# Decode attention on one core: K transposed by VectorE in blocks of bf16 pairs instead of on TensorE

## The chip, the cores and the metric

The kernel runs on one core of a Trainium2 chip. The time is device microseconds of one execution on that core. The engines are named as in the profile: PE (TensorE matmul), PEld (TensorE weight load), DVE (VectorE), ACT (ScalarE), POOL (GpSimd), SP (SyncE).

## What is computed

Softmax attention of one query position over 65,536 keys, with 32 query heads sharing 8 key heads, four to each, and head size 128, in bf16:

```python
B, Hq, Hkv, Sq, Sk, D = 1, 32, 8, 1, 65536, 128
k = jnp.repeat(k, rep, axis=1)          # rep = 4
v = jnp.repeat(v, rep, axis=1)
scores = jnp.einsum("bhqd,bhkd->bhqk", q, k) * D ** -0.5
p = softmax(scores, axis=-1)
out = jnp.einsum("bhqk,bhkd->bhqd", p, v)
```

K and V are 134.2 MB each and are read once. Each key takes part in four dot products and four weighted sums, so there is little arithmetic for each byte.

## The kernel before

K and V are cut into chunks of 128 x 64 keys (2 MB). Chunk i belongs to key head h = i // 8; partition p of a chunk holds 64 keys in a row (16 KB), so a tile is the t-th key of each of the 128 partitions, 128 keys x 128 elements. There are N = 64 chunks of K and as many of V, C = 8 to a head.

SP issues all loads in one order, worked out ahead (`merged`): K chunks run C chunks ahead of V chunks, and at the end V falls further behind. K has four buffers (NK), V six (NV). A K load waits until the chunk four back has been transposed (`tr_s`, L163), a V load until the values of the chunk six back are done (`pv_s`, L167). The first K chunk and the last V chunk come in pieces (FIRST, LAST).

For the scores PE needs the head dimension on the partitions, while a tile arrives with the keys there. So for each group of 8 tiles PE makes eight transposes into a PSUM bank (`trb`, L211), DVE or ACT copies the bank to SBUF (`ktb`; DVE L283, ACT L332, shared out by `on_act`), and PE makes eight matmuls with the transposed tile as weights and the four query columns as moving operand (`qkb`, L224). PE's order is written out in `pe_ops`: scores trail the transposes by three groups, and eight value matmuls (`PV`) go between. ACT moves a chunk's 256 columns of scores from PSUM to `scs` (L340), DVE takes their maximum for each query head (L287). After a head's last chunk DVE combines the maxima (L294), POOL reduces over partitions (L182), ACT scales the result (L344) and makes four exponentials into `pts`, with their sums (L353), and POOL sums over partitions (L184).

The values of a head add up in PSUM over its chunks: for heads 0 to 6 the V tile is the weight and four columns of `pts` move (L252); for head 7 `pts` is the weight and the V tile's 128 columns move (L254). DVE divides by the sum (L306; the last head L317). Heads 0 to 6 are transposed once on PE (L259) and stored from ACT's queue; head 7 is stored from SP's.

Of the kernel before, what the change touches and what calls it, by code (L numbers as in the profile page):

```python
# [1 line left out]

# [6 lines left out]
DT = mybir.dt  # L9
# [5 lines left out]
T = 64  # L15
TB = 8
G = T // TB
NK, NV = 4, 6
NTR = 4
NKT = 8  # L20
LAG = 3
FIRST = (16, 16, 32)
LAST = (32, 16, 8, 8)


def bass_standalone__gqa_softmax__decode_kernel(nc, q, k, v, out):
    B, Hq, Sq, D = q.shape
    _, H, Sk, _ = k.shape
    assert B == 1 and Sq == 1 and D == P and Hq % H == 0
    R = Hq // H  # L30
    CK = P * T
    assert Sk % CK == 0 and R * T <= 512 and Hq <= P
    C = Sk // CK
    TPH = C * T
    N = H * C
    scale = float(D) ** -0.5
# [5 lines left out]
    def merged(ahead):  # L42

        items = [(float(j), 0, ("K", j)) for j in range(N)]
        for i in range(N):
            back = 0.5 * max(0, i - (N - 2 * C)) if i < N - C else 0.5 * C
            items.append((i + C - ahead + back, 1, ("V", i)))
        return [it for _, _, it in sorted(items)]

    dma_seq, pe_seq = merged(0), merged(-1)  # L50


    pe_ops = []
    j = 0
    pend = []

    def tr(kg):
        pe_ops.append(("TR", kg))
        pend.append(kg)
        if len(pend) > LAG:  # L60
            pe_ops.append(("QK", pend.pop(0)))

    while j < len(pe_seq):
        kind, i = pe_seq[j]
        both = kind == "K" and j + 1 < len(pe_seq) and pe_seq[j + 1][0] == "V"
        last_k = kind == "K" and i == N - 1
        if kind == "K":
            for g in range(G):
                tr(i * G + g)
                if both and not last_k:  # L70
                    pe_ops.append(("PV", pe_seq[j + 1][1], g))
            if last_k:
                while pend:
                    pe_ops.append(("QK", pend.pop(0)))
                both = False
        else:
            for g in range(G):
                pe_ops.append(("PV", i, g))
        j += 2 if both else 1


    def on_act(kg):
        kc, g = divmod(kg, G)
        if kc < C:
            return g in (1, 4, 6)
        return kc % C >= 2 and g in (1, 5)

    n_act = [0]
    for kg in range(N * G):
        n_act.append(n_act[-1] + on_act(kg))  # L90
# [9 lines left out]
    ktb = [sb(f"ktb{i}", [P, TB * P], DT.bfloat16) for i in range(NKT)]  # L100
    scs = [sb(f"scs{i}", [P, TPH * R], DT.float32) for i in range(2)]
    pts = [sb(f"pts{i}", [P, TPH * R], DT.bfloat16) for i in range(2)]
    qsb = sb("qsb", [Hq, D], DT.bfloat16)
    qT = sb("qT", [P, Hq], DT.bfloat16)
    ident = sb("ident", [P, P], DT.bfloat16)
    identf = sb("identf", [R, R], DT.float32)
    hpart = sb("hpart", [P, 2 * C * R], DT.float32)
# [9 lines left out]
    orows = sb("orows", [Hq - R, D], DT.bfloat16)  # L117
    olast = sb("olast", [R, D], DT.bfloat16)
    warm = sb("warm", [P, 2], DT.float32)

    trb = [S(nc.psum_tensor(f"trb{i}", [P, TB * P], DT.bfloat16)) for i in range(NTR)]
    qkb = [S(nc.psum_tensor(f"qkb{i}", [P, 512], DT.float32)) for i in range(2)]
    pvb = [S(nc.psum_tensor(f"pvb{i}", [P, 512], DT.float32)) for i in range(2)]

    def sem(name):
# [6 lines left out]
    q_in, id_in, o_out = sem("q_in"), sem("id_in"), sem("o_out")  # L132
    tr_s, cpd_s, cpa_s = sem("tr_s"), sem("cpd_s"), sem("cpa_s")
    qk_s, sc_s, mx_s, hm_s = sem("qk_s"), sem("sc_s"), sem("mx_s"), sem("hm_s")
    hma_s, nb_s, ex_s, ls_s = sem("hma_s"), sem("nb_s"), sem("ex_s"), sem("ls_s")
    pv_s, rc_s, fin_s = sem("pv_s"), sem("rc_s"), sem("fin_s")
    qt_s, qT_s, idf_s, ot_s, or_s, warm_s = (
        sem("qt_s"), sem("qT_s"), sem("idf_s"), sem("ot_s"), sem("or_s"), sem("warm_s"))
# [10 lines left out]

    eye = nc.inline_tensor(np.eye(P).astype(ml_dtypes.bfloat16), name="eye").ap()  # L150
# [4 lines left out]
    def _(sp):  # L155
# [19 lines left out]
        sp.wait_ge(o_out, 32)  # L175

    @block.gpsimd
    def _(g):
        for h in range(H):
            hs = slice(h * R, (h + 1) * R)  # L180
            g.wait_ge(hm_s, h + 1)
            g.partition_all_reduce(hmaxa[:, hs], hmax[:, hs], P, bass.bass_isa.ReduceOp.max).then_inc(hma_s, 1)  # L182
            g.wait_ge(ex_s, R * (h + 1))
            g.partition_all_reduce(lsum[:, hs], rsum[:, hs], P, bass.bass_isa.ReduceOp.add).then_inc(ls_s, 1)  # L184

    @block.tensor
    def _(pe):
        def copied(kg):
            if on_act(kg):
                pe.wait_ge(cpa_s, n_act[kg + 1])  # L190
            else:
                pe.wait_ge(cpd_s, kg + 1 - n_act[kg + 1])

        pe.wait_ge(id_in, 16)
        pe.wait_ge(q_in, 16)
        pe.transpose(qkb[1][:, 0:Hq // 2].bitcast(DT.bfloat16), qsb[:, :], ident[0:Hq, 0:Hq]).then_inc(qt_s, 1)  # L196
        for op in pe_ops:
            if op[0] == "TR":
                kg = op[1]
                kc, g = divmod(kg, G)  # L200
                if kc == 0:
                    for n, a, b in pieces(FIRST):
                        if a == g * TB:
                            pe.wait_ge(first_in[n], 16)
                elif g == 0:
                    pe.wait_ge(k_in[kc % NK], 16 * (kc // NK + (kc % NK > 0)))
                if kg >= NTR:
                    copied(kg - NTR)
                for t in range(TB):
                    at = (g * TB + t) * D  # L210
                    ins = pe.transpose(trb[kg % NTR][:, t * P:(t + 1) * P], kbuf[kc % NK][:, at:at + D], ident[:, :])  # L211
                ins.then_inc(tr_s, 1)
            elif op[0] == "QK":
                kg = op[1]
                kc, g = divmod(kg, G)
                h = kc // C
                copied(kg)
                if kg == 0:
                    pe.wait_ge(qT_s, 1)
                if g == 0 and kc >= 2:  # L220
                    pe.wait_ge(sc_s, kc - 1)
                for t in range(TB):
                    at = (g * TB + t) * R
                    ins = pe.matmul(  # L224
                        qkb[kc % 2][:, at:at + R],
                        lhsT=ktb[kg % NKT][:, t * P:(t + 1) * P],
                        rhs=qT[:, h * R:(h + 1) * R],
                        start=True, stop=True,
                    )
                if g == G - 1:  # L230
                    ins.then_inc(qk_s, 1)
            else:
                _, i, g = op
                h, c = divmod(i, C)
                if g == 0:
                    if c == 0:
                        pe.wait_ge(ex_s, R * (h + 1))
                        if h >= 2:
                            pe.wait_ge(fin_s, h - 1)
                    if i < N - 1:  # L240
                        pe.wait_ge(v_in[i % NV], 16 * (i // NV + 1))
                if i == N - 1:
                    for n, a, b in pieces(LAST):
                        if a == g * TB:
                            pe.wait_ge(last_in[n], 16)
# [14 lines left out]


    side = []
    for op in pe_ops:
        if op[0] == "TR":
            side.append(("CP", op[1]))
        elif op[0] == "QK" and op[1] % G == G - 1:
# [123 lines left out]
```

## Time and profile before

Three executions took 655.04, 657.07 (the median) and 657.52 us. The profiled one:

| | |
|---|---|
| its own time | 654.79 us |
| its span, first to last instruction | 653.0 us |
| mean granted clock of PE | 0.658 |
| busy: PE, PEld | 606.0 us (93%), 602.4 us (92%) |
| busy: DVE, ACT, POOL | 313.6 us (48%), 178.5 us (27%), 6.6 us (1%) |
| instructions | 25,665, of them 12,290 matmuls |
| moved by DMA | 270.12 MB, 414 GB/s over the span |
| 2 MB loads, issue to landing | K 27.4 us, V 32.1 us (median) |
| SP's K loads waiting for transposes (`tr_s`) | 515.3 us in 60 waits, the longest 12.4 us |

How to read it. A page divides the span into 40 slices of 16.3 us; a digit is the busy share of a slice in tenths, and PEclk is the clock that was granted to PE, in tenths of full speed. A row of a group gives line, engine, operation, output and inputs, shape and count; then busy time and mean nanoseconds of one; then the idle time before it and what ended most of it. Durations of neighbours can overlap, so the distance between the starts of two instructions is read from the timeline (start, length, engine, line, operation). SP's waits cost nothing as long as loads issued earlier are still moving.

### The profile page before, as it was taken

What the parts mean: (1) busy time and instruction counts of PE and PEld (TensorE: products, weight loads), DVE (VectorE), ACT (ScalarE), POOL (GpSimd) and SP (SyncE); (2) the same over time, 40 slices, a digit from 0 to 9 for tenths busy, and PEclk for the clock granted to TensorE, in tenths of its full rate; (3) what the DMA queues carried; (4) which work ended last, traced back from release to release, by engine and by line L of the source; (5) the groups of instructions that cost most, each with busy time, mean ns of one, the idle gap of its engine ahead of it and who ended that gap; (6) DMA issues with size and microseconds to landing.
All of it is one profiled execution on the core that took longest, in us unless ns stands there. A gap on an engine that the chain in (4) does not pass through costs nothing.

```text
span 653.0 us, 25665 instructions
## 1 busy us (share of the span) xinstructions
PE 606.0 (93%) x12290; PEld 602.4 (92%) x12290; DVE 313.6 (48%) x497; ACT 178.5 (27%) x246; POOL 6.6 (1%) x20
## 2 busy tenths in 40 slices
PE   5987898998798989999999999999999999998798
PEld 5987898998798989999999999999999999988697
DVE  3666544564444734446444464444644446455200
ACT  3555122232222322223122231222312223132400
POOL 0000000000000000000000000000000000000000
PEclk9999858776866755555555555555555555597799
DMA  8999999999999999999999999999999999899995
GB/s 359 429 424 425 426 423 425 427 428 422 427 428 423 423 426 427 426 424 428 424 424 425 425 426 425 425 426 424 429 423 426 428 391 387 360 426 428 386 425 206
DMA packets 19497, 270.12 MB, mean 414 GB/s; under 512 B 2370, under 2 KB 2370, under 8 KB 3010
## 3 DMA queue, kind: packets, MB, share of 16 engines
q1 hardware_dynamic: 19160, 268.45, 97.4%
q8 instruction: 96, 1.57, 1.0%
q10 hardware_dynamic: 234, 0.05, 0.0%
q14 instruction: 7, 0.06, 0.0%
HBM read 268.48 MB, written 0.01 MB: 411 GB/s over the span
## 4 chain that ended last, share of the span: by engine, by line
PE 75%; DMA 20%; issue 3%; ACT 1%; DVE 1%; SPq 0%; POOL 0%; DVEq 0%
PE trb L211 49%; DMA kbuf<-in_k_dram 17%; PE pvb L252 12%; PE qkb L224 12%; DMA vbuf<-in_v_dram 3%; PE pvb L254 2%; ACT pts L353 1%; DVE ktb L283 1%; SPq L160 0%; DVE hpart L287 0%; SPq L164 0%; POOL hmaxa L182 0%; DVE olast L317 0%; DVE hmax L294 0%; ACT negb L344 0%
## 5 line engine op out<-in xcount | busy, mean ns | idle before, releaser
L211 PE MATMUL trb<-ident,kbuf 128*128 128x128 bf16 x4096 | 451.9, 279 | 20.3 <-DMA kbuf<-in_k_dram 15.0
L283 DVE COPY ktb<-trb 128x1024 bf16<-128x1024 bf16 x404 | 277.2, 690 | 289.3 <-PE trb L211 286.4
L211 PEld LDWEIGHTS trb<-ident,kbuf 128*128 128x128 bf16 x4096 | 342.4, 125 | 23.0 <-DMA kbuf<-in_k_dram 15.7
L332 ACT ACTIVATE ktb<-trb 128x1024 bf16<-128x1024 bf16 x108 | 110.6, 1024 | 348.5 <-PE trb L211 348.5
L224 PE MATMUL qkb<-qT,ktb 128*128 128x4 bf16 x4096 | 195.6, 170 | 7.5 <-issue 7.3
L224 PEld LDWEIGHTS qkb<-qT,ktb 128*128 128x128 bf16 x4096 | 194.7, 109 | 6.5 <-issue 6.1
L252 PE MATMUL pvb<-pts,vbuf 128*128 128x4 bf16 x3584 | 153.2, 166 | 9.9 <-issue 7.2
L252 PEld LDWEIGHTS pvb<-pts,vbuf 128*128 128x128 bf16 x3584 | 126.4, 102 | 11.3 <-issue 8.4
L340 ACT ACTIVATE scs<-qkb 128x256 f32<-128x256 f32 x64 | 24.5, 383 | 73.9 <-PE qkb L224 73.9
L353 ACT ACTIVATE pts<-scs,negb 128x512 bf16<-128x512 f32 x32 | 41.1, 1435 | 0.3
L287 DVE TENSOR_REDUCE hpart<-scs 128x4 f32<-128x256 f32 x64 | 38.9, 608 | 0.9 <-ACT scs L340 0.9
L254 PE MATMUL pvb<-vbuf,pts 128*4 128x128 bf16 x512 | 30.3, 223 | 1.5 <-DMA vbuf<-in_v_dram 0.9
L254 PEld LDWEIGHTS pvb<-vbuf,pts 128*4 128x4 bf16 x512 | 29.8, 87 | 1.9 <-DMA vbuf<-in_v_dram 1.1
L317 DVE TENSOR_SCALAR olast<-pvb,rcol 4x128 bf16<-4x128 f32 x1 | 0.3, 338 | 25.7 <-PE pvb L254 25.7
L182 POOL PARTITION_ALL_REDUCE hmaxa<-hmax x8 | 3.0, 372 | 564.5 <-DVE hmax L294 564.5
L353 ACT ACTIVATION_READ_ACCUMULATOR pts<-scs,negb 128x1 f32 x32 | 8.2, 255 | 0.0
L306 DVE TENSOR_TENSOR oT<-pvb,recip 128x4 bf16<-128x4 f32 x7 | 1.1, 161 | 10.4 <-PE pvb L252 10.2
L196 PE MATMUL qkb<-ident,qsb 32*128 32x32 bf16 x1 | 0.2, 181 | 5.6 <-DMA qsb<-in_q_dram 5.6
L196 PEld LDWEIGHTS qkb<-ident,qsb 32*128 32x128 bf16 x1 | 0.1, 97 | 5.6 <-issue 5.6
L344 ACT ACTIVATE negb<-hmaxa 128x4 f32<-128x4 f32 x8 | 1.6, 205 | 11.0 <-POOL hmaxa L182 11.0
L184 POOL PARTITION_ALL_REDUCE lsum<-rsum x8 | 3.4, 431 | 44.0 <-ACT pts L353 44.0
L309 DVE COPY orows<-trb 28x128 bf16<-28x128 bf16 x1 | 0.2, 214 | 5.5 <-PE trb L259 5.5
(14 smaller groups left out, 5.7 us busy)
## 6 DMA issues: line engine op xcount, KB each, us to landing
kbuf<-in_k_dram SPq DMA_DIRECT2D x63, 2048.0 KB, 27.4
vbuf<-in_v_dram SPq DMA_DIRECT2D x63, 2048.0 KB, 32.1
kbuf<-in_k_dram SPq DMA_DIRECT2D x2, 512.0 KB, 4.5
kbuf<-in_k_dram SPq DMA_DIRECT2D x1, 1024.0 KB, 7.1
vbuf<-in_v_dram SPq DMA_DIRECT2D x1, 1024.0 KB, 17.6
vbuf<-in_v_dram SPq DMA_DIRECT2D x1, 512.0 KB, 18.5
vbuf<-in_v_dram SPq DMA_DIRECT2D x2, 256.0 KB, 18.7
ident<-eye ACTq DMA_DIRECT2D x1, 32.0 KB, 3.2
```

The lines of the kernel that those rows point to most:

```text
L182: g.partition_all_reduce(hmaxa[:, hs], hmax[:, hs], P, bass.bass_isa.ReduceOp.max).then_inc(hma_s, 1)
L184: g.partition_all_reduce(lsum[:, hs], rsum[:, hs], P, bass.bass_isa.ReduceOp.add).then_inc(ls_s, 1)
L211: ins = pe.transpose(trb[kg % NTR][:, t * P:(t + 1) * P], kbuf[kc % NK][:, at:at + D], ident[:, :])
L224: ins = pe.matmul(qkb[kc % 2][:, at:at + R], lhsT=ktb[kg % NKT][:, t * P:(t + 1) * P], rhs=qT[:, h * R:(h + 1) * R], start=True, stop=True,)
L252: ins = pe.matmul(pvb[h % 2][:, 0:R], lhsT=v_t, rhs=p_t, start=st, stop=sp_)
L254: ins = pe.matmul(pvb[h % 2][0:R, 0:D], lhsT=p_t, rhs=v_t, start=st, stop=sp_)
L283: dv.tensor_copy(ktb[n % NKT][:, :], trb[n % NTR][:, :]).then_inc(cpd_s, 1)
L287: dv.tensor_reduce(hp[:, h % 2, c, :], scs[h % 2][:, c * T * R:(c + 1) * T * R].rearrange("p (t g) -> p g t", g=R), AX.X, ALU.max,).then_i ...
L332: ac.activation(ktb[n % NKT][:, :], trb[n % NTR][:, :], AF.Copy).then_inc(cpa_s, 1)
L340: ac.activation(scs[s][:, c * T * R:(c + 1) * T * R], qkb[n % 2][:, 0:T * R], AF.Copy).then_inc(sc_s, 1)
L344: ac.activation(negb[:, hs], hmaxa[:, hs], AF.Copy, scale=-scale).then_inc(nb_s, 1)
L353: ac.activation(pv[:, g_, :], sv[:, g_, :], AF.Exp, bias=negb[:, col], scale=scale, accum_out=rsum[:, col],).then_inc(ex_s, 1)
```

## The change

Chunks become 128 x 128 keys (4 MB, 32 KB in each partition): T = 128, N = 32 chunks, C = 4 to a head. K has two buffers, V three, of twice the size.

A group is now 16 tiles. DVE reads the group as int32, that is as pairs of bf16, and transposes it in one instruction of 128 x 1024 int32, block by block of 32 x 32, from SBUF to SBUF (`ktb`, four buffers). Within a quarter of 32 partitions the pairs of the head dimension come to lie on the partitions; the four quarters hold four different sets of keys. So a tile of `ktb`'s columns, taken every second bf16 (e = 0 or 1) and for each half b of the pairs, has 32 pair indices of four key sets on its 128 partitions. The query is spread into `qblk`, block-diagonal: for each head, b and e, 16 columns, of which the four columns of set a are non-zero only on quarter a. Four matmuls (b, e) add up to 16 columns of scores for 128 column positions. ACT then sorts the scores back: for each half chunk (a unit of 4 groups) sixteen moves, each from one quarter of `qkb` to one quarter of `scs`. `qkb` has six banks.

PE has no transposes and `trb` is gone; ACT makes no copies of K. PE makes a group's scores, then the 16 values of the V chunk that lies beside (`beside`), in order; the last five V chunks (`rest`) follow after all K. DVE waits for a unit's moves and takes the maximum after the second group of the next unit, and at the end of a head at once. POOL clears `qblk`, `oT` and `identf` at the start and makes the identity; the identity's load is gone, and q is loaded four times from ACT's queue, once into each quarter. Heads 0 to 6 are transposed at the end by DVE (`oX`) and stored in four pieces from ACT's queue.

The load order is now K0 K1 K2 V0 K3 V1 K4 V2 and so on to V23, and then K26 K27 V24 K28 K29 V25 K30 V26 K31 V27 V28 V29 V30 V31. A K load waits for the transposes of the chunk two back, a V load for the values of the chunk three back. Maximum, exponentials, values and division have the form they had, with the same number of exponentials and maxima.

```diff
-T = 64
-TB = 8
-G = T // TB
-NK, NV = 4, 6
-NTR = 4
-NKT = 8
-LAG = 3
-FIRST = (16, 16, 32)
-LAST = (32, 16, 8, 8)
+S4 = 32
+T = 128
+TG = 16
+G = T // TG
+U = 2
+GU = G // U
+NK, NV = 2, 3
+NKT = 4
+NQ = 6
+FIRST = (16, 16, 32, 64)
+LAST = (64, 32, 16, 8, 8)
...
+    def behind(i):
+        late = i - (N - 2 * C)
+        return i + C - 2 if late < 0 else min(N - 1, i + C - 2 + (1, 2, 2, 3)[min(late, 3)])
+
+    dma_seq = []
+    for j in range(N):
+        dma_seq.append(("K", j))
+        dma_seq += [("V", i) for i in range(N) if behind(i) == j]
...
+    for i in range(N):
+        j = max(free, i + C, behind(i) + 1)
+        if j < N:
+            beside[j] = i
+            free = j + 1
         else:
+            rest.append(i)
...
+        def scores(kg):
...
+            kt = ktb[kg % NKT][:, :].rearrange("p (b n e) -> p b e n", b=NB, e=NE)
+            pe.wait_ge(tr_s, kg + 1)
+            for n in range(TG // A):
+                at = (g % GU * (TG // A) + n) * A * R
+                for be in range(NB * NE):
+                    b, e = divmod(be, NE)
+                    qs = (h * NB * NE + be) * A * R
+                    ins = pe.matmul(
+                        qkb[u % NQ][:, at:at + A * R],
+                        lhsT=kt[:, b, e, n * P:(n + 1) * P],
+                        rhs=qblk[:, qs:qs + A * R],
+                        start=be == 0, stop=be == NB * NE - 1,
+                    )
+            ins.then_inc(qk_s, 1)
...
+        for kg in range(N * G):
+            kc, g = divmod(kg, G)
+            if kg % GU == 0 and kg // GU >= NQ:
+                pe.wait_ge(mv_s, kg // GU - NQ + 1)
+            scores(kg)
+            if kc in beside:
+                if g == 0:
+                    values_ready(beside[kc])
+                values(beside[kc], range(g * TG, (g + 1) * TG))
...
-                for t in range(TB):
-                    at = (g * TB + t) * D
-                    ins = pe.transpose(trb[kg % NTR][:, t * P:(t + 1) * P], kbuf[kc % NK][:, at:at + D], ident[:, :])
-                ins.then_inc(tr_s, 1)
...
+        def spread_q():
+
+            dv.wait_ge(q_in, 16 * A)
+            dv.transpose(qt[:, :].bitcast(DT.int32), q4[:, :].bitcast(DT.int32)).then_inc(qt_s, 1)
...
+            for a in range(A):
+                for b in range(NB):
+                    rows = slice(a * S4, (a + 1) * S4)
+                    dv.tensor_copy(to[rows, a, b, :, :, :], fr[rows, b, :, :, :]).then_inc(qb_s, 1)
...
+        def transpose(kg):
...
+            elif g == 0:
+                dv.wait_ge(k_in[kc % NK], 16 * (kc // NK + (kc % NK > 0)))
+            if kg >= NKT:
+                dv.wait_ge(qk_s, kg - NKT + 1)
+            fr = kbuf[kc % NK][:, g * TG * D:(g + 1) * TG * D].bitcast(DT.int32)
+            to = ktb[kg % NKT][:, :].bitcast(DT.int32)
+            dv.transpose(
+                to.rearrange("p (b t j) -> p b t j", b=NB, t=TG),
+                fr.rearrange("p (t b i) -> p b t i", b=NB, t=TG),
+            ).then_inc(tr_s, 1)
+
+        def maximum(u):
+            h, c = divmod(u, C * U)
+            dv.wait_ge(mv_s, u + 1)
...
-                dv.tensor_copy(ktb[n % NKT][:, :], trb[n % NTR][:, :]).then_inc(cpd_s, 1)
...
+            transpose(kg)
+            if kg % GU == 1 and todo:
+                maximum(todo.pop())
+            if kg % GU == GU - 1:
+                u = kg // GU
+                if u % (C * U) < C * U - 1:
+                    todo.append(u)
                 else:
+                    maximum(u)
...
-                ac.activation(ktb[n % NKT][:, :], trb[n % NTR][:, :], AF.Copy).then_inc(cpa_s, 1)
...
-                ac.activation(scs[s][:, c * T * R:(c + 1) * T * R], qkb[n % 2][:, 0:T * R], AF.Copy).then_inc(sc_s, 1)
...
+            ac.wait_ge(qk_s, (u + 1) * GU)
+            fr = qkb[u % NQ][:, 0:W].rearrange("p (n a g) -> p a n g", a=A, g=R)
+            to = scs[s][:, c * W:(c + 1) * W].rearrange("p (n x g) -> p x n g", x=A, g=R)
+            for x in range(A):
+                for a in range(A):
+                    ins = ac.activation(to[a * S4:(a + 1) * S4, x, :, :], fr[x * S4:(x + 1) * S4, a, :, :], AF.Copy)
+            ins.then_inc(mv_s, 1)
```

## The prediction

> **What bounds the kernel now.** I read the page first, for the share of each engine and the slices of the span.
>
> ```profile
> PEclk9999858776866755555555555555555555597799
> DMA  8999999999999999999999999999999999899995
> GB/s 359 429 424 425 426 423 425 427 428 422 427 428 423 423 426 427 426 424 428 424 424 425 425 426 425 425 426 424 429 423 426 428 391 387 360 426 428 386 425 206
> ...
> q1 hardware_dynamic: 19160, 268.45, 97.4%
> q8 instruction: 96, 1.57, 1.0%
> ```
>
> The transfers are the floor. From 16 us on nearly every slice moves about 425 GB/s with the DMA engines full. 270.12 MB at 425 are 635.6 us of the 653.0 us span, so only 17.4 us can be won by better cover. They lie in four places: the first slice (359: 16.3 x (1 - 359/425) = 2.5), slices 33 to 35 (5.2), slice 38 (1.4) and the last (206: 8.4).
>
> The stretch view (busy us of PE, PEld, DVE, ACT, POOL; granted clock; DMA share; GB/s) says why:
>
> ```profile
> 32.60:522.40 489.80, 462.68 (x9320) 460.49 (x9318) 248.08 (x388) 133.64 (x186) 4.82 (x12) 0.61 1.01 425
> 522.40:571.40 49.00, 49.00 (x918) 49.00 (x916) 25.72 (x41) 12.06 (x19) 0.80 (x2) 0.50 0.93 380
> ```
>
> PE is full at a granted clock of 0.50. The chain of waits there repeats one step, and the timeline splits it:
>
> ```profile
> 267.28 0.88 PE trb L211 x8
> 268.56 0.88 PE trb L211 x8
> ```
>
> ```profile
> 301.46 0.29 PEld L252 LDWEIGHTS pvb<-pts,vbuf 128*128 128x128 bf16 x8
> ...
> 301.68 0.77 PEld L211 LDWEIGHTS trb<-ident,kbuf 128*128 128x128 bf16 x8
> ```
>
> Every 1.28 us come eight transposes (0.88 us), eight scores and eight values (301.46 to 301.68, 0.22 us). 1.28 us is one 512 KB share of K and V, or 410 GB/s. PE is a little slower than the transfers, the buffers absorb it for 300 us, and then the loads wait. In the last slice PE finishes late and V waits for its buffers. The groups that the change touches:
>
> ```profile
> L211 PE MATMUL trb<-ident,kbuf 128*128 128x128 bf16 x4096 | 451.9, 279 | 20.3 <-DMA kbuf<-in_k_dram 15.0
> L283 DVE COPY ktb<-trb 128x1024 bf16<-128x1024 bf16 x404 | 277.2, 690 | 289.3 <-PE trb L211 286.4
> ...
> L332 ACT ACTIVATE ktb<-trb 128x1024 bf16<-128x1024 bf16 x108 | 110.6, 1024 | 348.5 <-PE trb L211 348.5
> ...
> L340 ACT ACTIVATE scs<-qkb 128x256 f32<-128x256 f32 x64 | 24.5, 383 | 73.9 <-PE qkb L224 73.9
> L353 ACT ACTIVATE pts<-scs,negb 128x512 bf16<-128x512 f32 x32 | 41.1, 1435 | 0.3
> L287 DVE TENSOR_REDUCE hpart<-scs 128x4 f32<-128x256 f32 x64 | 38.9, 608 | 0.9 <-ACT scs L340 0.9
> ```
>
> The timeline gives pitches, which durations hide:
>
> ```profile
> 58.95 2.47 DVE L283 COPY ktb<-trb 128x1024 bf16<-128x1024 bf16 x4
> ...
> 59.77 1.44 ACT L353 ACTIVATE pts<-scs,negb 128x512 bf16<-128x512 f32 x1
> 60.95 0.26 ACT L353 ACTIVATION_READ_ACCUMULATOR pts<-scs,negb 128x1 f32 x1
> 61.01 1.44 ACT L353 ACTIVATE pts<-scs,negb 128x512 bf16<-128x512 f32 x1
> ```
>
> [...] On ACT the next instruction starts 0.23 us before the last one's end.
>
> **Part 1, PE.** 4096 transposes go: 0.88/8 = 110 ns each at half clock, 450 us. 4096 score matmuls and 4096 value matmuls stay. Now four score matmuls add up into one result and stream 16 columns instead of 4. The eight value pairs in 0.22 us are 27.5 ns a pair at half clock. The scores' weight load now picks every second bf16, which the trace does not show. It can't gain; it costs nothing more (27.5 ns) to one column a cycle, as the transposes' 128 columns at 110 ns. [...] Sum: 4096 x 30 + 3584 x 27.5 + 512 x 57 (the last head's rate in the tail at full clock) = 251 us of 640. PE stops being a bound.
>
> **Part 2, DVE.** 404 copies (277 us) and 108 on ACT (111 us) go. In come 256 transposes of 128x1024 int32. This is the number the case hangs on, and no row shows a transpose. [...] I take one cycle an element: 1.067 + 0.06 = 1.13 us (256 x 1.13 = 289 us), with two cycles, 2.19 us, as the other end. Maxima stay 64 x 0.61 = 39 us.
>
> **Part 3, ACT.** 64 moves of 128x256 become 64 x 16 moves of 32 partitions x 64. By the rows at 256 and 1024 elements a PSUM read is 0.17 us + 0.835 ns an element: 222 ns each if nothing overlaps, 16 = 3.6 us. With the 0.23 us overlap of the exponentials, only the 55 ns of elements remain. [...] I take 130 ns, between the ends: 2.1 us for sixteen, 133 us in all.
>
> **Part 4, waits and buffers.** A 4 MB chunk takes 9.8 us, a K and V pair 19.7. The queue runs ... K(i+1), V(i-1), K(i+2), V(i). V(i) waits for the values of chunk i-3, which PE does beside K(i+1); K(i+3) waits for the transposes of K(i+1). So when K(i+1) has landed, 19.7 us of transfers are left, less 1.5 us from last byte to consumer and 2 us from issue to first byte (0.73 to about 2.5 at the start): 16.2 us of grace. Work: 8 x 1.13 = 9.0, two maxima 1.2, a wait for moves 0.5, the last group's scores and values 0.9, handshakes 0.2: 11.8. Slack 4.4 us, no gap.
>
> New waits: DVE waits for ACT's moves before each maximum; behind it stand the next transposes, and PE and SP wait for those. After six groups it comes two transposes later (2.3 us) against moves ready after 0.9 + 2.1 + 0.2; hence the 0.5 to 1. At a head's end it stands about 4 us, but the next K chunk is then still landing. The first values of a head wait for the exponentials. After landing: transposes and a maximum 10.1, scores 1.1, moves 2.3, and then as the timeline has it at 608 us, maxima 0.85, all-reduce and scaling 0.75, exponentials 5.1 = 20.2 us, against 19.7 + 1.1 + 0.6 = 21.4 for the next chunk's first scores. It just fits. DVE's waits for a free ktb or finished values end as PE follows.
>
> Start: the q copies (four loads on ACT's queue at about 0.4 us issue, landing 4.4 as the old one did), one transpose, eight copies at 0.17 put the first transpose near 9 us; K(0) done at about 19, K(2) issued 2 us ahead of need. I put 0.5 us (0 to 1.5). POOL's clears and the select lie under q's landing; ident's load goes. The four output stores of 28 rows and oX lie beside the last V chunks: nothing, or about 2 us each on ACT's queue if they were last, which they are not.
>
> Tail: after K(31) come V(27) to V(31), 49 us. Exponentials end 20 us after K(31), V(28) lands at 19.7. Then each V chunk waits whole: 128 x 57 ns = 7.3 us. V(30) lands 9.8 us before V(31), so PE ends 14.6 - 9.8 = 4.8 us after the last landing, where before ended 2.
>
> **Transfers.** Bytes stay 268.45 MB; instruction bytes fall with PE's count from 1.57 to about 1.1 MB. 133 transfers become 71, their small completion packets half. I take 427 GB/s (425 to 431): 269.6/427 = 631.4 us.
>
> **Sum.** 2.5 start + 631.4 + 0.5 + 1.5 landing + 4.8 tail + 2.1 output (PE's end 650.9 to 653.0) = 642.8 us span. The profiled execution took 654.79 for 653.0, so +1.8: 644.6, call it 644.5 us. The same execution lies 2.3 us under the median 657.07 of three, so 10 us of gain stands against about 2 of scatter.
>
> **Rivals.** Slower: the transpose takes two cycles an int32. At 2.19 us the work after landing is 17.5 + 1.2 + 0.9 + 0.2 = 19.8, 3.6 over the grace, a gap at every second chunk, 14 x 3.7 = 52; the start, where K(0) to K(2) come without V between, loses about 18 (K(2) and V(3)). With 5 us of spread among the head waits: 720 us. It begins to cost at (16.2 - 2.3)/8 = 1.74 us. [...]
>
> Slack eaten piece by piece: moves at 222 ns make DVE wait 2.5 us in each chunk, which shows where two K chunks follow each other late in the order: 648. With weight loads at 54 ns too, the first values of a head come late at every head: 660. Weight loads at 107 ns alone: a group costs PE 16 x (107 + 28) = 2.2 us, as the slow transpose: 700.
>
> Tail at half clock: if the 2.5 us pauses between V chunks let the clock fall to 0.50, the last head's values cost 107 ns, 13.7 us a chunk, 55 from the exponentials on: 665. Against: with such pauses the clock was 1.00 at 640 to 653.
>
> **How the numbers follow.** Transfers hidden as summed, 0.62 (own range 636 to 652: rate and start). Slack or tail lost, 0.20 (647 to 700). Slow transpose, 0.14 (720). Something dearer still, 0.04. About 0.5% is what a measurement of this kernel can tell from no change. Faster: 0.60 + 0.04 = 0.64; same: 0.02 + 0.06 = 0.08; slower: 0.10 + 0.14 + 0.04 = 0.28. The range 636 to 690 leaves out the slow transpose and the dearer cases.
>
> **What would show it.** Right: about 425 GB/s in every slice but first and last, transposes near 1.1 us apart, DVE busy about 330 us, PE 40 to 60%, the load queue waiting but never dry, a chain of DMA until PE's last 15 us. Wrong: transposes at 2 us, holes in the GB/s row at V(3), V(7), V(11), DVE waiting long for ACT's moves, weight loads of the scores over 50 ns apart, clock 0.50 in the tail.

## The result and the profile after

The kernel after takes 652.42 us (median of 4 runs, 651.45 to 653.14); beside it the kernel before took 656.38 (655.04 to 657.52). The ratio is 0.994, with a 95% interval from 0.9914 to 0.9965: faster by 0.6%. Forecast were 644.5 us. The sign is right and the time lies in the range, but the gain is 4 us where 12.6 were expected. The profiled execution of after took 652.83 us for a span of 651.0. The prediction's sum for that span was 642.8, so 8.2 us are to be found.

The page of after, first the span, the engines and the transfers:

```profile
span 651.0 us, 18101 instructions
...
PE 272.1 (42%) x8192; PEld 254.0 (39%) x8192; DVE 335.3 (52%) x356; ACT 263.6 (40%) x1098; POOL 7.4 (1%) x24
...
GB/s 371 309 449 420 434 429 421 438 425 432 425 425 425 438 418 411 439 421 432 429 404 427 435 423 420 419 432 425 427 434 401 437 427 388 403 431 421 431 422 170
...
q1 hardware_dynamic: 10232, 268.44, 97.0%
q8 instruction: 64, 1.05, 0.6%
```

PE fell from 93% to 42% busy. The page shows no clock row here; the granted clock is 1.00 in every stretch below. DVE's 335 us are the 330 that were forecast. What is wrong stands in the GB/s row: the second slice has 309, slices 34 and 35 have 388 and 403. The stretches (columns as before: busy us of PE, PEld, DVE, ACT, POOL; clock; DMA share; GB/s):

```profile
16.00:26.00 10.00, 3.68 (x101) 3.04 (x97) 7.93 (x9) 3.81 (x18) 0.00 (x0) 1.00 0.67 277
22.00:25.50 3.50, 1.12 (x32) 1.01 (x32) 3.46 (x4) 0.01 (x1) 0.00 (x0) 1.00 0.02 5
48.80:537.00 488.20, 194.46 (x6256) 180.83 (x6256) 260.04 (x266) 205.06 (x862) 4.82 (x12) 1.00 1.00 426
537.00:565.00 28.00, 10.64 (x352) 10.00 (x352) 16.02 (x19) 15.91 (x59) 0.80 (x2) 1.00 0.95 391
```

For 488 us the transfers run full at 426 GB/s, as forecast. But from 22 to 25.5 us next to nothing moves (5 GB/s; from 16 to 26 us the DMA share is 0.67, a loss of 3.3 us), and late, where two K chunks follow each other, 28 x (1 - 391/426) = 2.3 us are lost. The groups and the waits:

```profile
L254 DVE STREAM_TRANSPOSE ktb<-kbuf 128x1024 int32<-128x1024 int32 x256 | 297.7, 1214 | 146.4 <-DMA kbuf<-in_k_dram 142.0
L329 ACT ACTIVATE scs<-qkb 32x64 f32<-32x64 f32 x1024 | 219.5, 214 | 340.1 <-PE qkb L175 328.9
L175 PE MATMUL qkb<-qblk,ktb 128*128 128x16 bf16 x4096 | 150.5, 175 | 354.6 <-DVE ktb L254 347.5
...
L262 DVE TENSOR_REDUCE hpart<-scs 128x4 f32<-128x256 f32 x64 | 38.1, 595 | 122.3 <-ACT scs L329 122.3
```

The maxima (last row) are 38 us of work and 122 us of waiting for ACT's moves. The start in the timeline:

```profile
12.88 0.18 POOL L150 TENSOR_SCALAR_AFFINE_SELECT identf<-identf 4x4 f32<-4x4 f32 x1 [11.53 <-issue]
13.09 6.88 DVE L254 STREAM_TRANSPOSE ktb<-kbuf 128x1024 int32<-128x1024 int32 x6 [3.39 <-POOL identf L150]
...
18.41 3.60 ACT L329 ACTIVATE scs<-qkb 32x64 f32<-32x64 f32 x16 [14.32 <-PE qkb L175]
...
22.04 0.60 DVE L262 TENSOR_REDUCE hpart<-scs 128x4 f32<-128x256 f32 x1 [2.07 <-ACT scs L329]
```

Six transposes in 6.88 us: one follows another by (6.88 - 1.21)/5 = 1.13 us, exactly the value taken. Sixteen moves take 3.60 us, 226 ns each, where 2.1 us were taken. And the first transpose waits 3.39 us for POOL's select, before which POOL had done nothing for 11.5 us. The tail:

```profile
594.17 2.37 DVE L254 STREAM_TRANSPOSE ktb<-kbuf 128x1024 int32<-128x1024 int32 x2 [4.73 <-DMA kbuf<-in_k_dram]
...
617.60 31.35 PE L193 MATMUL pvb<-vbuf,pts 128*4 128x128 bf16 x512 [6.28 <-ACT pts L343]
649.05 0.34 DVE L290 TENSOR_SCALAR olast<-pvb,rcol 4x128 bf16<-4x128 f32 x1 [30.59 <-PE pvb L193]
```

K(31) is there at 594.2, the exponentials are done 23.4 us later (20.2 were forecast), and from then on PE works 31.35 us without a pause: no V chunk is waited for. The theory: the moves at 226 ns and the select make DVE late, so K's buffers come free late, holes open in the transfers, and the last head starts late. The rival: the transfers themselves are slower than the mean rate says, whatever DVE does.

### The profile page after: what moved, and what is told of

It reads as the page before. It is cut to its first block, busy times and chain, and to the rows that moved or that the text cites. A ratio compares the mean times of both kernels' runs of the same rounds, so it can differ in the third digit from the quotient of the medians.

```text
span 651.0 us, 18101 instructions
## 1 busy us (share of the span) xinstructions
PE 272.1 (42%) x8192; PEld 254.0 (39%) x8192; DVE 335.3 (52%) x356; ACT 263.6 (40%) x1098; POOL 7.4 (1%) x24
## 3 DMA queue, kind: packets, MB, share of 16 engines
q8 instruction: 64, 1.05, 0.6%
## 4 chain that ended last, share of the span: by engine, by line
DMA 49%; DVE 20%; ACT 16%; PE 9%; issue 4%; SPq 1%; POOL 0%; ACTq 0%; POOLq 0%; DVEq 0%
DMA kbuf<-in_k_dram 49%; DVE ktb L254 18%; ACT scs L329 13%; PE pvb L193 5%; PE qkb L175 3%; DVE hpart L262 2%; ACT pts L343 2%; PE pvb L191 1%; SPq L139 1%; POOL hmaxa L157 0%; ACTq L349 0%; DVE hmax L269 0%; ACT negb L334 0%; POOL qblk L146 0%; DVE olast L290 0%
## 5 line engine op out<-in xcount | busy, mean ns | idle before, releaser
L254 DVE STREAM_TRANSPOSE ktb<-kbuf 128x1024 int32<-128x1024 int32 x256 | 297.7, 1214 | 146.4 <-DMA kbuf<-in_k_dram 142.0
L329 ACT ACTIVATE scs<-qkb 32x64 f32<-32x64 f32 x1024 | 219.5, 214 | 340.1 <-PE qkb L175 328.9
L175 PE MATMUL qkb<-qblk,ktb 128*128 128x16 bf16 x4096 | 150.5, 175 | 354.6 <-DVE ktb L254 347.5
L175 PEld LDWEIGHTS qkb<-qblk,ktb 128*128 128x128 bf16 x4096 | 129.4, 105 | 371.7 <-issue 212.6
L191 PE MATMUL pvb<-pts,vbuf 128*128 128x4 bf16 x3584 | 126.0, 166 | 16.0 <-ACT pts L343 15.8
L191 PEld LDWEIGHTS pvb<-pts,vbuf 128*128 128x128 bf16 x3584 | 112.4, 104 | 16.7 <-ACT pts L343 16.5
L262 DVE TENSOR_REDUCE hpart<-scs 128x4 f32<-128x256 f32 x64 | 38.1, 595 | 122.3 <-ACT scs L329 122.3
L193 PEld LDWEIGHTS pvb<-vbuf,pts 128*4 128x4 bf16 x512 | 31.2, 89 | 6.4 <-ACT pts L343 6.4
L269 DVE TENSOR_REDUCE hmax<-hpart 128x4 f32<-128x32 f32 x8 | 1.6, 206 | 0.3
## 6 DMA issues: line engine op xcount, KB each, us to landing
kbuf<-in_k_dram SPq DMA_DIRECT2D x1, 2048.0 KB, 11.5
```

Source lines behind the costliest of these rows:

```text
L175: ins = pe.matmul(qkb[u % NQ][:, at:at + A * R], lhsT=kt[:, b, e, n * P:(n + 1) * P], rhs=qblk[:, qs:qs + A * R], start=be == 0, stop=be = ...
L191: ins = pe.matmul(pvb[h % 2][:, 0:R], lhsT=v_t, rhs=p_t, start=first, stop=final)
L193: ins = pe.matmul(pvb[h % 2][0:R, 0:D], lhsT=p_t, rhs=v_t, start=first, stop=final)
L254: dv.transpose(to.rearrange("p (b t j) -> p b t j", b=NB, t=TG), fr.rearrange("p (t b i) -> p b t i", b=NB, t=TG),).then_inc(tr_s, 1)
L262: dv.tensor_reduce(hp[:, h % 2, c, :], scs[h % 2][:, c * W:(c + 1) * W].rearrange("p (n g) -> p g n", g=R), AX.X, ALU.max,).then_inc(mx_s, 1)
L269: dv.tensor_reduce(hmax[:, h * R:(h + 1) * R], hp[:, h % 2, :, :].rearrange("p u g -> p g u"), AX.X, ALU.max,).then_inc(hm_s, 1)
```

## The experiments

The runs were made on several chips, and the kernel after was not run again beside them. A difference of some 2 us to its 652.42 could be one between chips, so such a difference counts here only with the place in the trace where it arises.

**The select out of the way.** DVE's wait for POOL's select goes from the start to the last head, where the identity is used:

```diff
         spread_q()
-        dv.wait_ge(init_s, 4)
...
             else:
+                dv.wait_ge(init_s, 4)
                 dv.tensor_tensor_reduce(
```

> DVE waits for POOL's select not before its first transpose but before the one place that uses the identity, at the very end. The changed kernel took 652.4 us. Theory of the start: the first transpose moves from 13.1 to 9.7 us, K(0) is released 3.4 us sooner, the hole before K(2) shrinks by as much, 649.0. Theory that the loss is only in the steady stretch and the tail: unchanged, 652.4 (the hole comes back before a later load).

650.30 us (649.5 to 651.26), span 649.1.

```profile
10.24 6.88 DVE L254 STREAM_TRANSPOSE ktb<-kbuf 128x1024 int32<-128x1024 int32 x6
...
592.29 2.37 DVE L254 STREAM_TRANSPOSE ktb<-kbuf 128x1024 int32<-128x1024 int32 x2 [5.10 <-DMA kbuf<-in_k_dram]
```

The first transpose starts 2.85 us sooner, and the hole at 22 us shrinks (369 GB/s from 16 to 26 us where 277 stood); K(31) is there 1.9 us earlier, and the end moves by the same 1.9. The late hole stays (388 GB/s from 537 to 565). So the select costs 1.9 us and not the 3.4 that were expected. What is left of the first hole comes from DVE's wait for the moves: with the late maximum as well (all mends, below) the same stretch moves 415 GB/s.

**One move instead of sixteen.** ACT moves a unit in one instruction of 128 x 256; the sorting between quarters is left out.

```diff
-            for x in range(A):
-                for a in range(A):
-                    ins = ac.activation(to[a * S4:(a + 1) * S4, x, :, :], fr[x * S4:(x + 1) * S4, a, :, :], AF.Copy)
-            ins.then_inc(mv_s, 1)
+            ac.activation(scs[s][:, c * W:(c + 1) * W], qkb[u % NQ][:, 0:W], AF.Copy).then_inc(mv_s, 1)
```

> The sixteen moves of a unit become one move of 128x256, as in the kernel before. It leaves out the sorting of the scores between the quarters, so the output is not the reference's; loads, transposes, matmuls and exponentials stay. Theory of the moves: DVE's wait for ACT before a maximum falls from 122 us to under 10, K(2) is issued about 2 us sooner, the holes near 540 and 562 us (2.3 us) go, and the last exponentials end 3.2 us sooner: about 645. Theory of the coarse grain (4 MB chunks, two and three buffers set the pace whatever ACT does): within 1 us of 652.4.

649.29 us (647.87 to 649.83), span 647.6. The waits (us in total, times, longest) and the late stretch:

```profile
DVE hpart L262 <- ACT scs L325: 12.8, 9, 3.0
```

```profile
537.00:565.00 28.00, 12.85 (x384) 11.58 (x384) 19.85 (x19) 5.38 (x12) 0.43 (x1) 1.00 1.01 430
```

122 us of waiting become 13 and the late hole is gone: it came from the moves. But the time misses the expected 645 by 4 us, since the end moved elsewhere. The tail now waits for V:

```profile
629.52 16.08 PE L193 MATMUL pvb<-vbuf,pts 128*4 128x128 bf16 x256 [2.40 <-DMA vbuf<-in_v_dram]
```

**Sixteen moves that stay in their quarter.** The moves have the same size, but each writes the quarter that it reads; the sorting is left out again.

```diff
-                    ins = ac.activation(to[a * S4:(a + 1) * S4, x, :, :], fr[x * S4:(x + 1) * S4, a, :, :], AF.Copy)
+                    ins = ac.activation(to[x * S4:(x + 1) * S4, a, :, :], fr[x * S4:(x + 1) * S4, a, :, :], AF.Copy)
```

> Each of the sixteen moves keeps its quarter: it reads quarter x of qkb and writes quarter x of scs, at the place a. It leaves out the sorting between quarters, so only the time is read. Question: is it the change of quarter that makes the moves follow each other at 226 ns (sixteen in 3.60 us, each 214 ns long), or the size of a move? If the change of quarter holds back the next move, sixteen take about 16 x 130 = 2.1 us, DVE waits some 40 us instead of 122 for them, and the time is 649 to 650. If a move of 32 x 64 from PSUM costs 226 ns wherever it goes, sixteen stay at 3.6 us, the wait at 122 us and the time at 652 to 653.

650.30 us (649.66, 650.95; on its chip the kernel before took 661.12), span 647.8. From the timeline:

```profile
305.10 2.20 ACT L329 ACTIVATE scs<-qkb 32x64 f32<-32x64 f32 x16 [3.61 <-PE qkb L175]
307.33 0.60 DVE L262 TENSOR_REDUCE hpart<-scs 128x4 f32<-128x256 f32 x1 [2.92 <-ACT scs L329]
```

Sixteen in 2.20 us, about as the prediction had it, and DVE's wait falls from 122.3 to 50.5 us (40 expected; the time lies just over the expected 649 to 650). The mean distance is (2.20 - 0.21)/15 = 133 ns at 206 ns each, but it hides two different ones. The first four moves, all in one quarter, take 0.53 us:

```profile
305.10 0.53 ACT L329 ACTIVATE scs<-qkb 32x64 f32<-32x64 f32 x4 [3.61 <-PE qkb L175]
```

That is (0.53 - 0.21)/3 = 107 ns. Over all 64 units the start times in the trace give 112 ns from one move to the next within a quarter, an overlap of 94 ns, and 217 ns from the last move of a quarter to the first of the next, with no overlap, although no move of this run crosses quarters. In the kernel after, where each move writes another quarter than the one before, the distance is 226 ns throughout, also ahead of the moves that stay in their quarter. So a move needs not cross quarters to lose the overlap: it is lost when the next move goes to another quarter. (Here source and destination change together; an order that keeps the destination for four moves while the source changes was not tried.) The 130 ns of the prediction are close to the 133 ns that this run has in the mean, and wrong for the order that the kernel has, with 226.

**The maximum two transposes later.** All sixteen moves stay; DVE asks for them after the fourth group of the next unit instead of the second.

```diff
-            if kg % GU == 1 and todo:
+            if kg % GU == GU - 1 and todo:
                 maximum(todo.pop())
```

> A unit's maximum is taken after the fourth group of the next unit instead of after the second, so that ACT's moves have 4.6 us instead of 2.3 before DVE asks for them. Theory of the moves in DVE's way: DVE's wait for ACT falls from 122 to about 40 us (only at the ends of heads), the start gains 2 us, the holes near 540 and 562 go, the tail stays: 648. Theory that the waits are hidden and the moves only count in the tail: 652.4.

649.04 us (648.6 to 649.38), span 646.8.

```profile
DVE hpart L262 <- ACT scs L329: 41.6, 12, 5.9
```

```profile
537.00:565.00 28.00, 11.88 (x384) 11.12 (x384) 20.95 (x23) 18.71 (x72) 0.80 (x2) 1.00 1.01 430
```

One changed condition hides two thirds of the wait and wins 4.2 us of span with the moves as slow as they were; 648 us were expected. K(31) is there at 589.91. As with one move, the tail then waits for V (`in_v_dram` releases PE at 630.36).

**Chunks of 2 MB.** T = 64, one unit to a chunk, four K and six V buffers, pieces and late order to match.

```diff
-T = 128
+T = 64
...
-U = 2
+U = 1
...
-NK, NV = 2, 3
+NK, NV = 4, 6
...
-FIRST = (16, 16, 32, 64)
-LAST = (64, 32, 16, 8, 8)
+FIRST = (16, 16, 32)
+LAST = (32, 16, 8, 8)
```

> The changed kernel with chunks of 2 MB (16 KB rows), four K buffers and six V buffers, as before; units, moves, transposes and the form of everything else stay. Theory of the coarse grain: K(0) to K(3) are issued at once, no hole at 22 to 26 us (4.4 us), none near 540 and 562 (2.3 us), the tail follows: 645.5. Theory that larger transfers pay for themselves (half the completions): the rate falls from 426 to 424 GB/s and 3 us of that are lost again, 648.5. Theory of the moves alone: 652.

650.71 us (649.97 to 652.26), span 648.5. The finer buffers leave no hole at the start (428 GB/s from 16 to 26 us), and yet the time is only 1.7 us shorter than with 4 MB, and none of the three expectations was met. The landing times in the trace show where the rest went. A load lands in sixteen parts, each with a time of its own. Of the last piece the first part is there at 632.7 us and the last at 644.1; in the kernel after it was 640.8 and 644.5. The first part gained 8 us, the last next to nothing, and the piece is there with its last. The runs of loads below look at this. In the trace a packet of 32 KB takes 1213 ns, two of 16 KB 1226 (medians), so the longer rows bring next to nothing here.

**Every transpose twice,** the first time into a spare tile:

```diff
+            if kg > 0:
+                dv.wait_ge(dup_s, kg)
+            dv.transpose(
+                ktw[:, :].bitcast(DT.int32).rearrange("p (b t j) -> p b t j", b=NB, t=TG),
+                fr.rearrange("p (t b i) -> p b t i", b=NB, t=TG),
+            ).then_inc(dup_s, 1)
```

> Every transpose of the changed kernel is made twice, the first into a spare tile, so DVE needs about 2.25 us for a group, as if the transpose took two cycles an element. Theory of the grace (16.2 us from a chunk's landing to the end of its last group): the work after landing is 18.0 + 1.2 + 0.9 + 0.2 = 20.3, 4.1 us over at every second chunk and about 18 at the start: 720 to 730. Rival, DVE's sum alone bounds (256 x 2.25 + 39 + waits): 690 to 700. Rival, transposes are hidden even then: 652.

738.10 us (two runs, 737.61 and 738.6), ratio to before 1.12 (1.111 to 1.1291). A group now costs DVE 2.26 us.

```profile
GB/s 372 191 432 428 426 207 340 428 321 439 331 425 426 333 425 333 427 347 407 433 331 423 322 425 405 360 430 324 426 324 438 435 238 327 329 426 410 223 418 156
```

A hole at every second K chunk, as the slow rival had it, which gave 720 for 2.19 us (720 to 730 expected for this run). Its mechanism holds, at a somewhat higher price; it did not happen in the kernel after because the transpose takes 1.13 us there and not 2.19.

**Loads alone, and loads beside PE.** With the holes mended, the tail still waited for V. So the loads were run by themselves, in a fixed ring of the five buffers, with zeros stored as the output and the whole computation left out; then with PE beside them, always the same matmul on a zeroed tile, so that PE moves no data of its own by DMA and adds only its instructions:

```diff
+            pe.wait_ge(k_in[n % bufs], 16 * (n // bufs + 1))
+            for m in range(128):
+                ins = pe.matmul(qkb[n % NQ][:, 0:16], lhsT=ktb[0][:, 0:P], rhs=qblk[:, 0:16], start=True, stop=True)
```

> The loads of K and V alone, in the same order and sizes, through five buffers; leaves out all of the computation, and stores zeros. Theory of the fetches: with almost no instructions to fetch, all sixteen queue engines end together, the increments of a chunk's landing stay within 3 us, and the span is 2.5 + 512 x 1.22 + 2 = 629. Rival (the memory or the engines themselves are uneven): eight of sixteen end 6 to 7 us later here too, span 640.

> The loads alone (span 627.0 us), and beside them PE makes 128 matmuls for each 4 MB chunk of K and V that lands, 8192 in all, always from the same zeroed tile. It leaves out the whole computation and stores zeros. No load waits for PE; PE adds nothing to the transfers but its own instructions, about 16,400, some 64 fetches of 16 KB as in the kernel after. Theory that the fetches all go to eight of the sixteen engines and make these late: 64 / 8 x 1.06 = 8.5 us, so a span of about 635 us, with the sixteen parts of the last large landing 6 to 8 us apart. Theory that the lateness comes from the waits of the loads for buffers, or from the small stores: span 627 to 628 and parts within 1 us.

> As the loads with PE beside them, with 256 matmuls for each chunk, 16,384 in all, about 128 fetches. It leaves out the whole computation. Theory of fetches on eight engines: 128 / 8 x 1.06 = 17 us over the loads alone, span about 644 us, and twice the lateness of the run with 128. Theory that fetches cost only their bytes, spread over sixteen engines: 2.1 MB at 427 GB/s = 5 us, span about 632. Theory that they cost nothing: 627 to 628.

Loads alone: 629.15 us, span 627.0. With 128 matmuls a chunk: 644.88, span 643.0. With 256: 756.15, span 755.2. The stretches of loads alone (busy POOL; clock; DMA share; GB/s):

```profile
320.00:618.00 298.00, 0.00 (x0) 1.00 1.00 431
618.00:624.00 6.00, 0.00 (x0) 1.00 0.98 421
624.00:627.00 3.00, 0.00 (x0) 1.00 0.03 3
```

The same with 128 matmuls a chunk (busy PE, PEld, POOL ahead of the clock):

```profile
320.00:618.00 298.00, 107.73 (x3850) 105.01 (x3851) 0.00 (x0) 1.00 1.00 429
618.00:624.00 6.00, 3.30 (x124) 3.21 (x121) 0.00 (x0) 1.00 0.92 396
625.00:636.00 11.00, 3.58 (x128) 3.49 (x128) 0.00 (x0) 1.00 0.49 207
```

Until 618 us both move nearly the same, 431 and 429 GB/s. Then loads alone stop at 624 with all engines at once, while beside PE half of the engines go on for another 12 us, a share of 0.49. The trace's landing times of the last 4 MB chunk's sixteen parts, sorted, say the same:

```
loads alone  624.4 624.5 624.5 624.5 624.6 624.6 624.6 624.6 624.6 624.6 624.7 624.7 624.7 624.8 624.9 625.0
128 a chunk  624.2 624.4 624.4 624.4 624.4 624.5 624.6 624.8 635.4 636.7 636.8 636.9 636.9 637.0 637.0 637.2
256 a chunk  624.2 624.4 624.4 624.5 624.5 624.6 624.7 624.9 642.9 642.9 643.0 643.1 643.2 643.3 643.3 644.7
```

Half of the engines go on and half of the parts are late, which reads as one engine to a part (an inference). Eight parts are on time to 0.2 us; the other eight are late by 11 to 12 us with 128 matmuls a chunk and by 18 to 20 with 256. PE waited for no data but these chunks, and no load waited for PE. What the page with 128 has among its transfers, and loads alone had not, is PE's instruction fetches, 64 packets with 1.05 MB for 16,384 matmuls and weight loads, so 16 KB and 256 instructions each:

```profile
q8 instruction: 64, 1.05, 0.7%
```

The lateness grows evenly with them. The mean of the late eight less that of the early eight is 0.2 us at the first landing, 5.7 at 294 us and 12.3 at 624 us, when 62 fetches had begun; with 256 a chunk it is 18.9 us, when 94 had. Spread over eight engines, both are 1.6 us a fetch, where its own packet takes 1.07 (1.03 in the kernel after, medians); so the lateness is larger than the 8.5 us expected. The trace does not name a packet's engine: that the fetches go by just the eight late ones is read from the landings. The rival, waits for buffers, expected 627 to 628 and is out for this program.

The run with 256 fell outside all three expectations, for another reason. Its waits, and its timeline:

```profile
PE qkb L128 <- issue: 281.6, 107, 4.0
```

```profile
304.23 3.58 PE L128 MATMUL qkb<-qblk,ktb 128*128 128x16 bf16 x128 [3.71 <-issue]
...
310.16 3.58 PE L128 MATMUL qkb<-qblk,ktb 128*128 128x16 bf16 x128 [2.34 <-issue]
...
317.17 3.58 PE L128 MATMUL qkb<-qblk,ktb 128*128 128x16 bf16 x128 [3.44 <-issue]
```

After each 128 pairs, one fetch of 256 instructions, PE stands 2 to 4 us and waits for nothing that the profile shows; that it waits for its own instructions is the reading that is left. Beside full load queues it gets 256 of them about every 6.5 us. The transfers end at 645 us, PE needs until 754, and with the queues empty it hardly stands any more (busy 95.5 of the 99 us from 655 on). In the kernel after, with a fetch every 651.0/64 = 10.2 us, PE has 0.2 us of such waits. At 6.5 it has 281.6 us of them, and with the late maximum already 31, in bursts. The transfers beside pay earlier: with 128 matmuls a chunk, a fetch every 643.0/64 = 10.0 us, eight of their parts come 12 us late.

**Every score matmul twice,** with the late maximum:

```diff
-            for n in range(TG // A):
+            for n in tuple(range(TG // A)) * 2:
```

> The kernel with the late maximum (649.0 us), each score matmul made twice, the second over the first; nothing else moves. PE gets 8192 more instructions and 110 us more work, of 388 us that it is idle. Theory of the fetches: about 32 more 16 KB instruction packets, all on eight engines, four on each at 1.05 us: the last landing 4.2 us later, and 0.5 us for the last group's second pass: 653.7. Rival (fetches are spread over sixteen engines and hidden, as the prediction had it): 649.5 to 650.5.

692.28 us (687.64 to 693.52): both theories missed. The waits show what neither had reckoned with, PE without instructions:

```profile
PE qkb L175 <- issue: 117.7, 51, 3.9
PE pvb L191 <- issue: 35.9, 14, 3.7
```

It came before the runs of loads with PE beside them, and led to them. It is no test of lateness, since PE was late with the values and the loads stood for it (slices of 286 to 344 GB/s).

**All mends together.** The select out of the way, the late maximum, and the last head in the form of the other seven (V as the weight, four columns moving), with one transpose of all heads and four stores at the end:

```diff
-                if h < H - 1:
-                    ins = pe.matmul(pvb[h % 2][:, 0:R], lhsT=v_t, rhs=p_t, start=first, stop=final)
-                else:
-                    ins = pe.matmul(pvb[h % 2][0:R, 0:D], lhsT=p_t, rhs=v_t, start=first, stop=final)
+                ins = pe.matmul(pvb[h % 2][:, 0:R], lhsT=v_t, rhs=p_t, start=first, stop=final)
```

> Three mends at once: DVE doesn't wait for POOL's select, the maximum comes after the fourth group of the next unit, and the last head's values take V as the weights like the others (28 ns a tile instead of 57), with one transpose and four stores for all heads at the end. Theory of the fetches (the last landing is set by the eight DMA queues' engines that also fetch instructions): the hole at the start goes (1.5 us against the late maximum alone), PE ends 0.5 us after the last landing instead of about 5; last landing near 639, span 643, time 645. Rival (the tail is bound by PE's form of the last head only): span 640.

643.39 us (642.91 to 645.72), ratio to before 0.9769 (0.972 to 0.9818): the best of all, 9 us under the kernel after. Its span of 641.0 lies between those of the two theories, 643 and 640, and does not decide between them. Its tail:

```profile
632.50:636.00 3.50, 2.84 (x94) 2.67 (x95) 0.00 (x0) 0.00 (x0) 0.00 (x0) 1.00 0.50 197
```

```profile
637.72 0.37 PE L191 MATMUL pvb<-pts,vbuf 128*128 128x4 bf16 x8 [0.25 <-DMA vbuf<-in_v_dram]
```

PE now works within 0.4 us of the last landing, and what it waits for is again half of the engines (share 0.50). Of the sixteen parts of the last piece, eight land from 631.1 to 632.3 and eight from 635.9 to 637.7.

**Fewer instructions.** In the kernel with all mends the values of heads 0 to 6 are made four tiles at a time, to have fewer fetches:

```diff
+            if h < H - 1:
+                for t in tiles[::VW]:
+                    tau = c * T + t
+                    ins = pe.matmul(
+                        pvb[h % 2][0:VW * R, 0:VW * D],
+                        lhsT=pts[h % 2][:, tau * R:(tau + VW) * R], rhs=vbuf[i % NV][:, t * D:(t + VW) * D],
+                        start=tau == 0, stop=tau == TPH - VW,
+                    )
```

> The kernel with all three mends (643.39 us, span 641.0), and the values of heads 0 to 6 made four tiles at a time: the sixteen columns of pts are the weight, 512 columns of V move, and at the end of a head four small matmuls pick the four useful blocks out of the 16 x 512 result. 896 pairs take the place of 3584, so some 5,400 of PE's instructions go, about 21 of 64 fetches. PE's time for them grows: 896 x 0.23 = 206 us where 3584 x 0.03 = 108 stood, still under 60% of the span. Theory that each fetch costs its transfer engine about 1.5 us (12.2 us of lateness for 64 fetches on eight engines in the loads with PE): 21 / 8 x 1.5 = 4 us off, span 637, time 639 to 640. Theory that in the full kernel the lateness comes from the loads' waits for buffers and not from the fetches: span 641, time 643 to 644. If PE's clock falls with the longer streams and PE becomes late: 650 or more.

652.26 us (651.28 to 654.11), the third case. From its page:

```profile
PE 413.3 (63%) x5532; PEld 207.9 (32%) x5532; DVE 339.6 (52%) x362; ACT 264.5 (41%) x1098; POOL 7.5 (1%) x24
...
PEclk9999978876988767887588875888758889668975
...
GB/s 360 435 424 436 430 421 417 434 429 424 345 435 428 434 417 379 438 422 439 414 356 432 414 417 430 358 433 431 433 394 367 425 439 423 407 420 444 417 437 275
```

The mean clock falls to 0.805, and four wide matmuls take 1.03 us in some stretches and 1.88 in others. At the starts of heads the loads wait for PE's values, and holes of some 2 to 3 us open, near 171, 253, 333, 415 and 497 us. The fetches fell to 43, and the parts of the last landing lie 2.7 us apart instead of 6.6. But the late parts may catch up in each hole, as in the kernel before, where the lateness fell from 15.0 to 4.7 us between 545 and 621 us in steps, where the loads stood; so this run does not show whether fewer fetches help.

## Why the prediction was right in sign and short in size

**PE (part 1): right.** The clock is 1.00, and sixteen scores with their weight loads take 0.57 to 0.60 us, sixteen values 0.57 (128 values in a row 3.58, 28 ns a pair). So taking every second bf16 costs next to nothing. No row of before stood behind the 30 ns taken for that weight load; in after sixteen such pairs take at most 0.03 us more than sixteen with contiguous weights.

**DVE (part 2): right.** 1.13 us a transpose, on which the case hung. No run shows the cycle, the 1.067 and the 0.06 us from which the value was put together, nor two cycles as the other end; what after shows is 1214 ns for one of 1024 int32, 245 for the one of 64, and 1.13 us from start to start. Doubled, it brings the holes of the slow rival, at 738 us.

**ACT (part 3) failed.** "I take 130 ns, between the ends: 2.1 us for sixteen": it is 226 ns and 3.6 us, the upper end that was named (222 ns), because each move goes to another quarter than the one before. The 130 was an estimate between two ends, and no run shows it for this order. With that, part 4's "hence the 0.5 to 1" is 2.07 us of waiting at mid-unit, and "It just fits" for the last head is 3.2 us late. The rival that the slack is eaten piece by piece had just this row, moves at 222 ns, with DVE waiting 2.5 us in each chunk and holes where two K chunks follow each other late, at 648 us. It was the mechanism that came true.

**Start failed:** "POOL's clears and the select lie under q's landing". The select runs at 12.88 us, with 11.5 us before it in which POOL waited for nothing that the profile shows. "I put 0.5 us (0 to 1.5)"; the loss was 3.3, of it 1.9 of span from the select.

**Transfers: nearly right, for the wrong reason.** "427 GB/s" is a mean over sixteen engines of which eight run ahead. A chunk counts as landed with its slowest part. In the kernel with all mends the last piece landed at 637.7, where the prediction's terms give 2.5 + 631.4 + 0.5 + 1.5 = 635.9; eight of its parts were there by 632.3, and PE's last eight values start at 637.72. So the term is about 2 us short, not more.

**The account of the 8.2 us.** The end of after hangs on K(31), the exponentials and PE. By the prediction K(31) is there at 635.9 - 49 = 586.9; it was 594.2, 7.3 late: 3.3 - 0.5 = 2.8 of it from the start, 2.3 from the late hole, and 2.2 are what is left. That rest is not the moves': with all mends, where neither hole is left, K(31) still comes at 588.8, 1.9 us behind the sum. Late engines are the likely cause, but their share was not measured. The exponentials took 23.4 instead of 20.2: 3.2. PE took 31.35 from there to its end at 648.95; the prediction had (642.8 - 2.1) - (586.9 + 20.2) = 33.6, with waits for V: 2.3 back. 7.3 + 3.2 - 2.3 = 8.2. That the tail fits in sum (PE ended 4.5 us behind the last landing, forecast 4.8) is chance: it was bound by PE and not by V.

The mends agree with this in size: 1.9 us of span for the select, 4.2 for the late maximum, 10.0 for both with the last head's new form. (Each compares one profiled execution; those of the kernel after span 649.6 to 651.3.) That brings 643.4 us, near the 644.5 forecast, but partly by a tail that the prediction left as it was.

**Open:** how much of the lateness in the full kernels is fetches, and how much the waits of the loads take back. In the kernel before it grew as evenly as beside PE alone, to 15.0 us at 536 us after 79 fetches (1.5 us a fetch on eight engines), and fell when the loads stood. With 64 fetches it was 12.3 us at the end beside PE alone, 9.5 in the last piece with 2 MB chunks, 5.9 with all mends and 1.8 in the kernel after. Why these differ was not followed up.

## What to carry to other kernels

Price a small instruction by its distance in the timeline from a neighbour with the same pattern of partitions: an overlap seen on full tiles (0.23 us on ACT before) may vanish when the next instruction goes to another quarter (112 ns from move to move within one, 217 to 226 between). When an engine is freed, look for who waits in order on another's last instruction; a later place for the wait (one changed condition here, 4 us) may do as much as a faster instruction. In a kernel bound by its transfers, ask when the slowest part of a chunk lands and not only for the mean GB/s, and count the instructions: with 64 of their fetches beside the loads, half of the parts came 12 us late.

## What the runs showed of the hardware that was not expected

- 64 instruction fetches (16 KB, 256 instructions) put eight of the sixteen parts of a load 12 us behind (span 627.0 to 643.0). Beside full load queues PE gets one about every 6.5 us. The kernel before has 96 in 653 us, one every 6.8; whether that held it back beside the clock was not tried.
- ACT's moves of 32 x 64 follow each other at 112 ns while they stay in one quarter of the partitions, and at 217 to 226 ns when the next one goes to another.
- PE's granted clock did not go by its busy share alone: 0.658 in the kernel before at 93% busy, 0.805 with 512-column streams at 63%, but 1.00 at over 80% for the last 110 us of the loads with 256 matmuls a chunk (16 columns, a zeroed tile); what sets it was not tried. On one chip the spans of the kernel before ran from 652.9 us (clock 0.634) to 661.2 (0.587); four of the kernel after, at 1.00, lie within 1.7 us.
- POOL's first select ran 10.6 to 12.2 us after its clears in the ten kernels that have it, with no wait that the profile shows.
